# Longformer attention and a softplus MLP: narrow idle products at the start, and weight loads that wait for earlier ones

## The chip, the cores and the metric

The kernel runs on one core of a Trainium2 chip. The metric is device time in microseconds (us): the median over several runs. A separate profiled execution gives the trace from which everything else is read. An instruction is named by its engine and its line in the kernel: PE is TensorE (PEld its weight loads), DVE VectorE, ACT ScalarE, POOL GpSimd, SP SyncE, which here only issues transfers.

## The reference

Batch 8, 8 heads, 576 positions, head size 64, 8 global positions drawn at random; then 4608 tokens of width 512 go through an MLP of width 2048.

```python
mask = np.abs(pos[:, None] - pos[None, :]) <= 32          # a band
mask = mask | is_global[:, None] | is_global[None, :]     # and global rows and columns
attn = softmax(where(mask, q @ k.T / sqrt(64), -1e9))
x = (attn @ v)  -> [4608, 512]
out = softplus(x @ w_in) @ w_out                          # w_in 512 x 2048, w_out 2048 x 512
```

All inputs are float32; the kernel computes in bf16 with float32 sums.

## The kernel before, in words

**Tiling.** The tokens are cut into 9 tiles of 512 (`m`), each tile into 4 groups (`n`) of 4 blocks of 32 positions. For a group, PE computes scores `s` for all 8 heads against the block's own, previous and next block and the global keys (`sc`, L1085), DVE takes the row maxima `m`, ACT the exponentials `st` (L1121 for the first four groups, in pieces of 128 columns), DVE the reciprocal of the sums, POOL or DVE the normalisation `pn` (L1140), DVE a transposition `pt` (L1149), and PE the product with v, `xo` (L1259). ACT and DVE copy `xo` to `xT`. Then PE computes `h` = xT times w_in (L1294, 16 chunks `c` of 128 columns of w_in), ACT the softplus `g` (L1300), and PE the product `o` with w_out (L1305). Of tile 0, `xo` and `h` come in three pieces of 128, 256 and 128 tokens. Once a batch, rows of the global positions are computed apart: `sg` (L976), exponentials `pg` (L988), `ov` (L1005), `vg`.

**Start of the program.** q and k of batches 0 and 1 come in three parts each: part 0 and 1 hold 256 positions (one transfer of 512 KB, L522), part 2 the last 64 (two transfers of 64 KB, L526); they are called q0, q1, q-tail, k0, k1, k-tail here. They are issued on SP's queue. A part is cast to bf16 (`qb`, `kb`), transposed by PE (`tr`, L865, in order q0, q-tail, q1 and k0, k1, k-tail), gathered at the global positions by PE (`pick`, L871), and the transposed tiles are copied to `qx` and `kx`. The scores of the first group need q0, k0 and, through the global keys that ACT copies from `pick`, all of k. v of batch 0 (8 transfers of 72 KB, L477) and w_in (8 transfers of 256 KB, called pieces 0 to 7, two for each of four tiles `win`, L1356) are issued on POOL's queue; they are cast on the way. POOL's queue is in order: an instruction that waits holds those behind it. Two of its instructions do nothing but wait: a copy of one column to `seen`. SP's queue waits in the same way before the loads of batch 1: a tiny transfer `trail` (L765) reads an element of `win`.

**Idle products.** Until PE has work, it multiplies a zeroed tile, `warm` (L737). `keep` puts such products into every gap of over 700 ns that the planner foresees in the first 34 us, and computes their number from a share of the gap and the duration of one.

**What sets the order.** `_Order` plans all jobs with costs written in the code. The table `ORDER` gives the order in which it takes them, five times the job's number plus the engine (0 PE, 1 ACT, 2 DVE, 3 POOL, 4 SP's transfers). The planner's times choose the idle products and sort the jobs; each engine then executes its instructions in that order. It also has a model of PE's instruction fetch (`stall`): blocks of 256 instructions, each asked for when a row of PE's program 318 ahead of its first is reached (`ASK`, `NEED`).

Of the kernel before, what the change touches and what calls it, by code (L numbers as in the profile page):

```python
# [20 lines left out]
class _Order:  # L21
# [16 lines left out]
    SWITCH = 107  # L38
# [4 lines left out]
    SLOW = ((27000, 8000), (34500, 6200), (55000, 8200), (230000, 6000), (1e9, 4500))  # L43
    NEAR = 150

    def stall(self, t, took, ins):
# [4 lines left out]
        while n + ins >= min(asked, need):  # L51
            at = min(asked, need)
            here = t + held + took * max(at - n, 0) / max(ins, 1)
            if at == asked:
                due.append(here)
                asked += self.BLOCK
            else:
                ask = due.pop(0)
                took_ = max(next(x for until, x in self.SLOW if ask < until), self.backlog(ask + 1200) - ask + 2400)
                last = max(ask + took_, last + self.FETCH)  # L60
                held += max(0, last - here)
                need += self.BLOCK
# [48 lines left out]
    BEGIN = 3300  # L111
# [43 lines left out]
    FILL, FILLT, NARROW, NFILL, NFILLT = 0.75, 220, 0, 0.8, 140  # L155
    COLD, COLDT, LONG = 5400, 427, 0.93
# [3 lines left out]
    def keep(self, t0, t1, order):  # L160
# [11 lines left out]
        if t0 < self.COLD:  # L172
            span = (t1 - t0) * self.LONG
# [20 lines left out]
    def due(self, j):  # L194

        t = j["hold"]
        for d in j["deps"]:
            same = d["on"] in j["cost"] and (
                d["on"] == "PE" or d["on"] == "DMA" and (not d["moves"] or not j["moves"] and d["cost"]["DMA"][0])
                or d["on"] == "POOL" and d["moves"])  # L200
# [10 lines left out]
    def run(self, free):  # L211
# [12 lines left out]
        dma = []  # L224
# [3 lines left out]
        while ready:  # L228
# [57 lines left out]
            if j["moves"]:  # L286
                mine = "POOL" if "POOL" in j["cost"] else "SP"
                dma.append((mine, t + 1500 if j["cost"][e][0] else t, j["moves"], j))
# [28 lines left out]
def kernel(  # L317
# [51 lines left out]
    ORDER = (52, 57, 62, 162, 167, 122, 137, 146, 156, 4, 117, 113, 151, 141, 132, 127, 182, 172, 177, 187, 370, 9, 14, 213,  # L369
# [1108 lines left out]
```

## Time and profile before

| | us |
|---|---|
| median of 3 runs (332.8 to 333.18) | 333.17 |
| profiled execution | 331.16 |
| its span, first to last instruction | 329.1 |
| PE busy in the span | 319.9 |
| idle products `warm`: 46, busy | 13.9 |
| first product `xo` of tile 0 starts at | 26.30 |
| first product `h` of tile 0 starts at | 28.20 |

The profiled execution took 2.06 us more than its span, and 2.01 us less than the median of the runs. Rows of the timeline below read: start in us, us, engine, line, operation, output<-inputs, shapes, number of instructions merged; in brackets the idle time of the engine before it and what ended it ("issue": nothing that the profile shows). Rows of the windows read: stretch, its length, busy us of each engine with the number of instructions, then the granted TensorE clock (1.00 is full), the share and the GB/s of the transfers. Rows of a queue read: packets, MB, share of 16 transfer engines' time; q1 carries SP's loads, q0 POOL's transfers, q8 blocks of PE's instructions.

### The profile page before, as it was taken

What the parts mean: (1) busy time and instruction counts of PE and PEld (TensorE: products, weight loads), DVE (VectorE), ACT (ScalarE), POOL (GpSimd) and SP (SyncE); (2) the same over time, 40 slices, a digit from 0 to 9 for tenths busy, and PEclk for the clock granted to TensorE, in tenths of its full rate; (3) what the DMA queues carried; (4) which work ended last, traced back from release to release, by engine and by line L of the source; (5) the groups of instructions that cost most, each with busy time, mean ns of one, the idle gap of its engine ahead of it and who ended that gap; (6) DMA issues with size and microseconds to landing.
All of it is one profiled execution on the core that took longest, in us unless ns stands there. A gap on an engine that the chain in (4) does not pass through costs nothing.

```text
span 329.1 us, 12101 instructions
## 1 busy us (share of the span) xinstructions
PE 319.9 (97%) x5290; PEld 171.3 (52%) x5290; DVE 219.9 (67%) x386; ACT 233.8 (71%) x459; POOL 196.0 (60%) x175
## 2 busy tenths in 40 slices
PE   8878999999999999999999999999999999999996
PEld 3536876565555444544555445445544454454444
DVE  7796689847997799884995975378776970431000
ACT  5698879676798896488558857995749647914622
POOL 7827828996678567969587496738282927230000
PEclk9997999999999999999999999999999999999999
DMA  7998999999889899999999960370010012001002
GB/s 193 187 205 195 198 189 155 157 166 244 136 152 146 152 226 173 180 228 189 178 179 167 155 162 4 127 145 3 4 66 0 36 66 85 13 32 66 34 32 97
DMA packets 168796, 42.14 MB, mean 128 GB/s; under 512 B 153256, under 2 KB 165800, under 8 KB 168744
## 3 DMA queue, kind: packets, MB, share of 16 engines
q1 hardware_dynamic: 155928, 27.15, 46.8%
q0 software_dynamic: 10944, 11.08, 16.9%
q10 hardware_dynamic: 1872, 3.15, 2.5%
q8 instruction: 41, 0.67, 0.9%
q14 instruction: 11, 0.09, 0.1%
HBM read 36.71 MB, written 9.44 MB: 140 GB/s over the span
## 4 chain that ended last, share of the span: by engine, by line
PE 90%; DVE 2%; SPq 2%; DMA 2%; issue 1%; ACT 1%
PE o L1305 39%; PE h L1294 37%; PE xo L1259 4%; PE s L1085 4%; DMA stage<-in_q_dram 2%; PE ov L1005 2%; SPq L522 1%; PE pick L894 1%; SPq L526 1%; PE sg L976 1%; PE warm L737 1%; DVE qx L728 1%; PE tr L865 1%; DVE m L1100 1%; PE pick L907 1%
## 5 line engine op out<-in xcount | busy, mean ns | idle before, releaser
L1305 PE MATMUL o<-wout,g 128*128 128x512 bf16 (+1 forms) x592 | 138.3, 374 | 0.0
L1294 PE MATMUL h<-xT,win 128*128 128x512 bf16 (+3 forms) x768 | 137.8, 328 | 0.1
L1300 ACT ACTIVATE g<-h 128x512 bf16<-128x512 f32 (+3 forms) x192 | 84.5, 503 | 30.0 <-PE h L1294 27.0
L1140 POOL TENSOR_TENSOR pn<-st,rs 128x1024 bf16<-128x1024 f32 (+1 forms) x38 | 66.7, 1766 | 55.7 <-DVE rs L1134 49.9
L1294 PEld LDWEIGHTS <-win 128*128 128x128 bf16 x768 | 67.5, 99 | 59.6 <-issue 0.8
L1305 PEld LDWEIGHTS <-g 128*128 128x128 bf16 x592 | 55.9, 98 | 60.7 <-ACT g L1300 1.0
L1108 POOL TENSOR_TENSOR st<-st,m 128x1024 f32<-128x1024 f32 x32 | 60.2, 1894 | 27.1 <-DVE m L1102 27.0
L1089 DVE TENSOR_TENSOR st<-s,mask 128x512 f32<-128x512 f32 x64 | 41.1, 677 | 18.6 <-PE s L1085 18.4
L1132 DVE TENSOR_REDUCE sm<-st 128x8 f32<-128x1024 f32 x32 | 38.5, 1203 | 14.8 <-ACT st L1125 14.6
L1102 DVE TENSOR_REDUCE m<-st 128x8 f32<-128x1024 f32 x32 | 37.9, 1209 | 0.3
L728 ACT COPY osb<-o 128x512 f32<-128x512 f32 (+1 forms) x30 | 17.2, 577 | 22.6 <-PE o L1305 20.2
L1125 ACT ACTIVATE st<-st 128x1024 f32<-128x1024 f32 x32 | 32.7, 1052 | 0.3
L1149 DVE STREAM_TRANSPOSE pt<-pn 128x512 int32<-128x512 int32 x36 | 24.5, 690 | 5.2 <-POOL pn L1140 5.1
L728 ACT CAST xT<-xo 128x512 bf16<-128x512 f32 (+3 forms) x28 | 11.7, 467 | 18.8 <-PE xo L1259 18.8
L728 DVE CAST xT<-xo 128x512 bf16<-128x512 f32 (+3 forms) x20 | 11.3, 601 | 17.5 <-PE xo L1259 17.4
L1300 ACT ACT_TABLE_LOAD x15 | 19.2, 1283 | 1.7 <-PE h L1294 1.5
L1125 ACT ACT_TABLE_LOAD x14 | 18.0, 1283 | 0.7 <-ACT osb L728 0.4
L725 POOL TENSOR_SCALAR qb<-stage 128x1152 bf16<-128x1152 f32 (+2 forms) x15 | 16.8, 1126 | 2.2 <-issue 1.1
L1085 PE MATMUL s<-kx,qx 64*32 64x128 bf16 x1152 | 14.5, 220 | 3.6 <-issue 2.8
L1085 PEld LDWEIGHTS <-qx 64*32 64x32 bf16 x1152 | 10.4, 90 | 12.2 <-issue 8.9
L728 POOL CAST vb<-stage 128x1152 bf16<-128x1152 f32 x12 | 13.7, 1146 | 3.3 <-DMA stage<-in_v_dram 3.3
L737 PE MATMUL warm<-vb 128*128 128x512 bf16 x46 | 13.9, 451 | 1.3 <-DVE vb L559 1.3
(127 smaller groups left out, 287.2 us busy)
## 6 DMA issues: line engine op xcount, KB each, us to landing
stage<-in_v_dram SPq DMA_DIRECT2D x56, 144.0 KB, 4.2
stage<-in_q_dram SPq DMA_DIRECT2D x48, 144.0 KB, 3.7
stage<-in_k_dram SPq DMA_DIRECT2D x48, 144.0 KB, 4.0
out_dram<-osb POOLq DMA_DIRECT2D x24, 256.0 KB, 3.2
out_dram<-osb ACTq DMA_DIRECT2D x11, 256.0 KB, 2.0
stage<-in_q_dram SPq DMA_DIRECT2D x4, 512.0 KB, 6.2
stage<-in_k_dram SPq DMA_DIRECT2D x4, 512.0 KB, 6.9
win<-in_moe_w_in_dram POOLq DMA_DIRECT2D x8, 256.0 KB, 7.7
```

What stands on the lines that cost most here:

```text
L728: {"ACT": nc.scalar.copy, "DVE": V.tensor_copy, "POOL": nc.gpsimd.tensor_copy}[e](out, in_)
L1085: nc.tensor.matmul(out=PS["s", n, g][quad(a), x, :], lhsT=qx[b % 2][rows(g), a, j * BL:(j + 1) * BL], rhs=kx[b % 2][rows(g), a, e0 * BL:(e ...
L1089: V.tensor_tensor(out=PS["st", n][:, h, :, :], in0=PS["s", n, h][:, :, :], in1=mask[:, h, j0:j0 + PB, :, :].rearrange("p j s i -> p j (s i ...
L1102: V.reduce_max(out=m[:], in_=flat(PS["st", n], h0, h1), axis=AX)
L1108: on(e).tensor_tensor(out=t, in0=t, in1=over(PS["m", n, y][:], SL * BL), op=OP.subtract)
L1125: nc.scalar.activation(out=t, in_=t, func=AF.Exp)
L1132: V.reduce_sum(out=sm[:], in_=flat(PS["st", n], h0, h1), axis=AX)
L1140: on(e).tensor_tensor(out=PS["pn", n][:, :, :, h0:h1].rearrange("p x s h -> p h x s"), in0=PS["st", n][:, h0:h1], in1=PS["rs", n, y][:].re ...
L1149: V.transpose(out=bass.AP(base.tensor, base.offset, ap=[list(base.ap[0]), [2 * STEP, PB // 2], [STEP + BL // 2, 2], [1, SL * BL]]), in_=PS ...
L1294: nc.tensor.matmul(out=h[:, :], lhsT=w_in_t[c // 4][:, kd, c % 4 * P:(c % 4 + 1) * P], rhs=PS["xT", m][:, kd, lo:hi], start=(kd == 0), sto ...
L1300: nc.scalar.activation(out=PS["g", m, c][:, lo:hi], in_=PS[key][:, lo_of(c, hi - lo)], func=AF.Softplus)
L1305: nc.tensor.matmul(out=PS["o", m, ns, a][:, :], lhsT=PS["g", m, kf][:, ns * P:(ns + 1) * P], rhs=w_out_t[kf // 4][:, kf % 4, a:z], start=( ...
```

## The change

1. The idle products of a gap that begins before 3 us are 128 columns wide instead of 512: the first series is 156 of 128 columns instead of 29 of 512.
2. POOL waits for k1 (a copy to `seen`) before it issues the first v.
3. Each of w_in's pieces 4 to 7 waits for the landing of the piece four before it, by a copy of one column of `win` to `seen` on POOL; the planner's fixed hold of 2000 ns on these transfers is gone.
4. SP's loads of batch 1 wait for the first piece of win2 (piece 4) instead of its second; w_out waits for k0 of batch 1 instead of k1.
5. Several of the planner's costs are changed, and `ORDER` is another table.

```diff
-    SWITCH = 107
+    SWITCH = 96
-    SLOW = ((27000, 8000), (34500, 6200), (55000, 8200), (230000, 6000), (1e9, 4500))
+    SLOW = ((27000, 6500), (36500, 5500), (50000, 7500), (230000, 5800), (1e9, 4500))
-    BEGIN = 3300
+    BEGIN = 2900
-    FILL, FILLT, NARROW, NFILL, NFILLT = 0.75, 220, 0, 0.8, 140
-    COLD, COLDT, LONG = 5400, 427, 0.93
+    FILL, FILLT, NARROW, NFILL, NFILLT = 0.75, 220, 3000, 0.93, 57
+    COLD, COLDT = 5400, 107
...
-                dma.append((mine, t + 1500 if j["cost"][e][0] else t, j["moves"], j))
+                dma.append((mine, t + (1900 if mine == "POOL" else 1500) if j["cost"][e][0] else t, j["moves"], j))
...
-    ORDER = (52, 57, 62, 162, 167, 122, 137, 146, 156, 4, 117, 113, 151, 141, 132, 127, 182, 172, 177, 187, 370, 9, 14, 213,
+    ORDER = (24, 29, 73, 78, 83, 88, 57, 176, 181, 62, 67, 152, 187, 192, 157, 14, 138, 217, 162, 197, 202, 312, 147, 33,
...
+    DEPTH = 4
...
-    seen = const([P, 2, 1], FP32, "seen")
+    seen = const([P, 10, 1], FP32, "seen")
...
+            last = o.add(pool(190), lambda e: nc.gpsimd.tensor_copy(seen[:, 2, :], natural(1, 1)[:, 0, 0, 0, 0:1]), [T["part", 0, 1, 1]], rank=0)
...
-            T["part", b, w, t] = o.add({"DMA": (700 if b else 0, 0)}, emit, had(("w_in", 2)) + T["cast", 0, w] if b else [], rank=0,
+            T["part", b, w, t] = o.add({"DMA": (700 if b else 0, 0)}, emit, had(("w_in", 2, 0)) + T["cast", 0, w] if b else [], rank=0,
...
+    pieces = []
     for x in range(4):
         for y in range(2):
-            last = T["w_in", x] = o.add({"POOL": (650, 0)}, lambda e, x=x, y=y: weights_in(x, y), [last or T["held"]],
-                                        rank=-1 if x else 0, hold=2000 if x else 0, moves=1340)
+            gate = []
+            if len(pieces) >= DEPTH:
+                n = len(pieces) - DEPTH
+                gate.append(o.add(pool(190), lambda e, n=n: nc.gpsimd.tensor_copy(seen[n % 2 * D:n % 2 * D + D, 4 + n, :], w_in_t[n // 2][n % 2 * D:n % 2 * D + D, 0, 0:1]), [pieces[n]], rank=0, late=1))
+            last = T["w_in", x] = T["w_in", x, y] = o.add({"POOL": (650, 0)}, lambda e, x=x, y=y: weights_in(x, y), [last or T["held"], *gate],
+                                        rank=-1 if x else 0, moves=1340)
+            pieces.append(last)
```

What the new table does to the order is seen best on two queues. First SP's queue, the first loads of the program. The transfers from `in_q_dram` and `in_k_dram` of 128x8x128 are parts 0 and 1, those of 64x4x64 the tails. Before:

```order
L531 DMA gi_63<-in_global_idx_dram 128x16
L522 DMA stage0_60<-in_q_dram 128x8x128
L522 DMA stage1_61<-in_k_dram 128x8x128 x2
L522 DMA stage0_60<-in_q_dram 128x8x128
L526 DMA stage1_61<-in_k_dram 64x4x64 x2
L526 DMA stage0_60<-in_q_dram 64x4x64 x2
L765 DMA trail_111<-win2_126 1x2x1
```

With the change:

```order
L533 DMA gi_63<-in_global_idx_dram 128x16
L528 DMA stage0_60<-in_q_dram 64x4x64 x2
L524 DMA stage0_60<-in_q_dram 128x8x128
L524 DMA stage1_61<-in_k_dram 128x8x128 x2
L524 DMA stage0_60<-in_q_dram 128x8x128
L528 DMA stage1_61<-in_k_dram 64x4x64 x2
L767 DMA trail_111<-win2_126 1x2x1
```

By the table's numbers the parts came as q0, k0, k1, q1, k-tail, q-tail, and come now as q-tail, q1, k1, k0, q0, k-tail. PE's order of transposes still begins with q0.

Second POOL's queue behind its first constants, up to the normalisation. Before:

```order
L725 TENSOR_SCALAR qb_64<-stage0_60 128x2x4x64
L477 DMA vb0_66<-in_v_dram 32x18x64 x8
L1373 COPY seen_110<-stage0_60 128x1
L1356 DMA win0_124<-in_moe_w_in_dram 64x4x512 x2
L671 COPY mask_78<-mask_78 128x2x256
L1356 DMA win1_125<-in_moe_w_in_dram 64x4x512 x2
L1356 DMA win2_126<-in_moe_w_in_dram 64x4x512 x2
L1356 DMA win3_127<-in_moe_w_in_dram 64x4x512 x2
L1140 TENSOR_TENSOR pn_735<-st_415,rs_680 128x512
```

With the change, up to the gate of piece 6:

```order
L1376 COPY seen_110<-stage0_60 128x1
L1359 DMA win0_124<-in_moe_w_in_dram 64x4x512 x2
L1359 DMA win1_125<-in_moe_w_in_dram 64x4x512
L667 MEMSET mask_78 128x9x32 x4
L775 COPY seen_110<-stage1_61 128x1
L478 DMA vb0_66<-in_v_dram 32x18x64 x2
L649 TENSOR_SCALAR mask_78<-near_120 128x2x9x8 x2
L730 CAST kb_65<-stage1_61 128x2x4x64
L478 DMA vb0_66<-in_v_dram 32x18x64 x2
L1383 CAST seen_110<-win0_124 64x1 x2
L478 DMA vb0_66<-in_v_dram 32x18x64 x2
L1359 DMA win1_125<-in_moe_w_in_dram 64x4x512
```

Three pieces of w_in are now issued ahead of v, and as soon as q1 has landed; the eight transfers of v are spread in pairs, the last two pairs behind the landing of pieces 0 and 1. Behind these rows come the last pair of v, the gates on pieces 2 and 3 and the issue of pieces 4 to 7, and then six normalisations `pn`. On ACT, the exponentials of groups 1 and 2 stand ahead of the first copy of `xT`, those of group 3 behind it, and then softplus; the product `vg` moves from ACT to DVE. PE has 12 idle products of 512 columns in later gaps (9 and 3) instead of 17 in six series.

More of the change, by code (lines that the diff above doesn't have):

```diff
@@ L58, in stall @@
                 ask = due.pop(0)
-                took_ = max(next(x for until, x in self.SLOW if ask < until), self.backlog(ask + 1200) - ask + 2400)
+                took_ = max(next(x for until, x in self.SLOW if ask < until), self.backlog(ask + 1400) - ask + 2400)
                 last = max(ask + took_, last + self.FETCH)
@@ L172, in keep @@
         if t0 < self.COLD:
-            span = (t1 - t0) * self.LONG
+            span = (t1 - t0) * share
             cold = min(span, self.COLD - t0)
@@ L199, in due @@
                 d["on"] == "PE" or d["on"] == "DMA" and (not d["moves"] or not j["moves"] and d["cost"]["DMA"][0])
-                or d["on"] == "POOL" and d["moves"])
+                or d["on"] == "POOL" and d["moves"] and (j["moves"] or not j["late"]))
             t = max(t, j["hold"] + (d["at"] if same else d["end"] + self.HOP))
@@ L759, with follow @@
     followed = set()
-    def follow(x, t):
+    def follow(x, t, row):
         if x in followed:
@@ L764, in follow @@
         followed.add(x)
-        nc.sync.dma_start(out=trail[x:x + 1, :], in_=t[D:D + 1, t.shape[1] - 1, t.shape[2] - 2:])
+        nc.sync.dma_start(out=trail[x:x + 1, :], in_=t[row:row + 1, t.shape[1] - 1, t.shape[2] - 2:])
     def add_load(b, w, deps):
@@ L775, in add_load @@
                     last = T["half", 0, h] = o.add({"POOL": (1300, 0)}, lambda e, h=h, x=x: load_v(nc.gpsimd, 0, h, range(2 * x, 2 * x + 2)), [last], rank=0,
-                                                   moves=1200, late=200)
+                                                   moves=1080, late=200)
                     T["cast", 0, 2].append(last)
@@ L782, in emit @@
                     if behind:
-                        follow(1, w_out_t[0])
+                        follow(1, w_out_t[0], D)
                     load_v(nc.sync, b, h, range(R))
@@ L795, in emit @@
                 if b:
-                    follow(0, w_in_t[2])
+                    follow(0, w_in_t[2], 0)
                 load_part(b, w, t)
-            T["part", b, w, t] = o.add({"DMA": (700 if b else 0, 0)}, emit, had(("w_in", 2)) + T["cast", 0, w] if b else [], rank=0,
-                                       moves=(1800 if b else 1900) if t < FULL else 900 if b else 650, units=1 if t < FULL else 2)
+            T["part", b, w, t] = o.add({"DMA": (700 if b else 0, 0)}, emit, had(("w_in", 2, 0)) + T["cast", 0, w] if b else [], rank=0,
+                                       moves=1800 if t < FULL else 900 if b else 650, units=1 if t < FULL else 2)
     def add_cast(b, w):
@@ L1042, in add_global @@
             ovs.append(o.add({"PE": (72 * n, 72 * n + 170) if b else (110 * n + 100, 110 * n + 240)}, lambda e, m0=m0, m1=m1: ov(e, m0, m1), [tps[-1], *ovs, *T["cast", b, 2]],
-                             rank=3, array=32, ins=16 * n, opens=[] if ovs else [("ov", ("ov", b, y)) for y in range(two)], uses=[("ov", b, y) for y in range(two)] if ovs else []))
+                             rank=3, array=34, ins=16 * n, opens=[] if ovs else [("ov", ("ov", b, y)) for y in range(two)], uses=[("ov", b, y) for y in range(two)] if ovs else []))
         T["gexp", b], T["tpg", b], T["ov", b] = exps[-1], tps[-1], ovs[-1]
@@ L1275, in add_values @@
             last = o.add({"PE": (t, t + 170)}, lambda e, s0=s0, s1=s1: val(e, s0, s1), ready if last is None else [last] + (had(("gv", 0)) if ahead else []),
-                         rank=1, array=64, urgent=last is None, ins=16 * (s1 - s0) + (8 if ahead and s0 == 0 else 0), opens=opened if last is None else [],
+                         rank=1, array=65, urgent=last is None, ins=16 * (s1 - s0) + (8 if ahead and s0 == 0 else 0), opens=opened if last is None else [],
                          uses=[("pt", m)] + ([("xo", v_, r) for r in range(KD)] if last is not None else []))
@@ L1436 @@
             make_batch(1)
-            T["landed"] = o.add(pool(100), lambda e: nc.gpsimd.tensor_copy(seen[:, 0, :], natural(1, 1)[:, 0, 0, 0, 0:1]), [T["part", 1, 1, 1]], rank=0)
+            T["landed"] = o.add(pool(100), lambda e: nc.gpsimd.tensor_copy(seen[:, 0, :], natural(1, 0)[:, 0, 0, 0, 0:1]), [T["part", 1, 1, 0]], rank=0)
             for a in range(KF // 4):
                 T["w_out", a] = o.add({"POOL": (800, 0)}, lambda e, a=a: weights_out(a),
-                                      [T["landed"], T.get(("w_out", a - 1))], rank=-1, hold=800 if a else 0, moves=2700)
+                                      [T["landed"], T.get(("w_out", a - 1))], rank=-1, moves=2700)
         for x in range(len(VALS)):
```

143 rows, old and new, of the table ORDER are left out of this document.

## The prediction

> **What bounds the kernel now.** I read the page first, then stretches of the span, then the first 40 us engine by engine, then the transfer queues.
>
> ```profile
> PE 319.9 (97%) x5290; PEld 171.3 (52%) x5290; DVE 219.9 (67%) x386; ACT 233.8 (71%) x459; POOL 196.0 (60%) x175
> ...
> 23.30:26.14 2.84, 0.00 (x2) 0.00 (x1) 2.13 (x8) 2.84 (x17) 0.62 (x1) 1.00 1.16 194
> 26.14:30.00 3.86, 3.86 (x74) 2.89 (x75) 2.10 (x6) 2.79 (x17) 3.42 (x4) 0.56 0.69 185
> 30.00:34.34 4.34, 4.34 (x141) 3.75 (x139) 3.20 (x7) 3.94 (x17) 2.65 (x3) 1.00 0.91 214
> 34.34:326.00 291.66, 291.26 (x4732) 154.09 (x4728) 193.59 (x309) 207.84 (x361) 173.94 (x130) 1.00 0.62 120
> ```
>
> PE bounds it. From 34.34 us on PE is idle 0.40 us in 291.66, so the time is the moment at which PE becomes full plus a fixed rest. All that can be won lies ahead of that moment: PE stands still for 2.84 us, and for the next 3.86 us has a clock of 0.56, which loses 3.86 x 0.44 = 1.7 us.
>
> ```profile
> 22.89 0.41 PE L1085 MATMUL s<-kx,qx 64*32 64x128 bf16 x30
> 26.14 0.23 PE L1085 MATMUL s<-kx,qx 64*32 64x128 bf16 x2 [2.84 <-issue]
> ...
> 28.20 4.33 PE L1294 MATMUL h<-xT,win 128*128 128x128 bf16 x60
> ...
> 34.34 0.39 PE L865 MATMUL tr<-ident,kb 128*128 128x128 bf16 x4
> ...
> 35.64 2.78 PE L1294 MATMUL h<-xT,win 128*128 128x256 bf16 x24
> ```
>
> The stop is in the middle of one group's scores and waits for nothing in the program. It is at row 704 of PE's program (scores at rows 644 to 707, 30 pairs done), where the planner's model of the instruction fetch has a block begin (448 + 256). The queue of PE's instructions shows one block moved between 23.5 and 24.0 us, none between 17.5 and 23.5:
>
> ```profile
> q8 instruction: 1, 0.02, 11.2%
> ...
> win<-in_moe_w_in_dram POOLq DMA_DIRECT2D x2, 256.0 KB, 9.7
> ```
>
> The second row is the last two of w_in's transfers (issued by 18.41, landing 9.7 us on): all eight had been queued in 6 us, and the block went through among them. I take the stop for that block.
>
> Beside PE runs a second chain, ACT's:
>
> ```profile
> 16.14 0.37 ACT L1121 ACTIVATE st<-s,m 128x128 f32<-128x128 f32 x1
> ...
> 20.31 0.35 ACT L1121 ACTIVATE st<-s,m 128x128 f32<-128x128 f32 x1
> ...
> 27.50 0.60 ACT L728 CAST xT<-xo 128x128 bf16<-128x128 f32 x3 [1.07 <-PE xo L1259]
> 27.98 0.39 ACT L1121 ACTIVATE st<-s,m 128x128 f32<-128x128 f32 x1
> ...
> 30.93 1.28 ACT L1300 ACT_TABLE_LOAD   x1
> 32.23 1.64 ACT L1300 ACTIVATE g<-h 128x128 bf16<-128x128 f32 x9
> 34.23 0.37 ACT L728 CAST xT<-xo 128x256 bf16<-128x256 f32 x1 [0.38 <-PE xo L1259]
> ```
>
> From the first exponential at 16.14 ACT is nearly full up to softplus; it lost only 1.07 us to PE's stop. So removing the stop does not give 4.5 us: ACT comes next.
>
> **The change part by part.** Call E the start of the first exponential. With the change ACT does, in order: group 0 and the global rows (16.14 to 20.31, 4.17), groups 1 and 2 (20.31 to 26.43 less `vg`, now on DVE: 5.9), two copies of xT (0.4), group 3 (27.98 to 30.93: 2.9), the table (1.28), four softplus (4 x 1.64/9 = 0.7), two copies of 256 columns (0.6). That is 16.0 us; then PE can begin `h` of 256 columns, at E + 16.0. Before, it began at 35.64, behind four groups of transposes of batch 1 in 1.30 us; the new order has only two ahead of it, so the equal point is 35.64 - 0.65 = 34.99. The gain is 34.99 - 16.0 - E = 19.0 - E. PE itself would be ready: `xo` of group 0 waits for POOL's normalisation behind w_in's last issue. Here is its price, and how long POOL needs to issue six pieces:
>
> ```profile
> 14.73 3.68 POOL L1356 DMA_DIRECT2D win<-in_moe_w_in_dram  x6
> 25.52 4.04 POOL L1140 TENSOR_TENSOR pn<-st,rs 128x512 bf16<-128x512 f32 x4 [7.11 <-DVE rs L1134]
> ```
>
> Piece 3 is issued behind the landing of piece 1 (14.9 by the packet rates below) and two issues of v (5.59 / 8 each), at 16.5. Landed at some 21, then three issues of 0.61: the first `pn` at 23, `xo` at 26, before ACT is at the copies (E + 10.1). This cover is about 2 us; if w_in's gates open later than that, every further us is lost. The gates and the fetch go together: with at most some four pieces outstanding the block no longer meets eight, PE does not stop for it, and the clock has no gap of 2.84 us. I cost the gates' copies (0.2 each on POOL) at nothing under the same cover, and the three added changes of tile shape on PE at 0.3 at most.
>
> So everything hangs on E, and E on two loads. The first parts became usable like this:
>
> ```profile
> 5.54 0.63 ACT L721 ACTIVATE qb<-stage 128x512 bf16<-128x512 f32 x1 [0.65 <-DMA stage<-in_q_dram]
> ...
> 7.35 1.14 ACT L728 CAST kb<-stage 128x512 bf16<-128x512 f32 x2 [1.18 <-DMA stage<-in_k_dram]
> ...
> 9.18 1.14 ACT L728 CAST kb<-stage 128x512 bf16<-128x512 f32 x2 [0.69 <-DMA stage<-in_k_dram]
> ...
> 12.69 0.74 DVE L728 COPY qx<-tr 128x512 bf16<-128x512 bf16 x1 [0.22 <-PE tr L865]
> ...
> 14.85 0.46 PE L1085 MATMUL s<-kx,qx 64*32 64x128 bf16 x32
> ...
> 15.41 1.29 DVE L1100 TENSOR_REDUCE m<-s 128x4 f32<-128x512 f32 x2
> ...
> L728 DVE CAST kb<-stage x4: 273/418/1275, 13.3 to 33.6; 128x512 bf16<-128x512 f32 x3, 128x256 bf16<-128x256 f32 x1
> ```
>
> (The last row groups the casts by DVE: least, median and longest in ns.) One part per 1.8 us. Now q-tail goes ahead (two transfers, 0.8 together), and q0, which PE's transposes need first, is fourth of the large ones: 5.54 + 0.8 + 3 x 1.8 = 11.8. Behind q0: two casts on DVE (0.85), first transposes (0.85), a copy (0.74), a cast (0.4), two copies (1.5), scores (0.46), maxima (0.65), hops: 5.7. So undisturbed loads give E = 17.5, against 16.14 before: the first exponential is later than now in any case. The gain is then 1.5.
>
> The loads are not undisturbed: w_in's pieces 0 to 2 are issued from 6.6 us, when k0, q0 and k-tail are still to come. What POOL's transfers do to SP's is seen in five stretches, from 8 to 9, 9 to 10, 10 to 11, 54 to 55 and 56 to 57 us:
>
> ```profile
> q1 hardware_dynamic: 580, 0.29, 120.4%
> ...
> q1 hardware_dynamic: 526, 0.27, 109.4%
> q0 software_dynamic: 100, 0.01, 20.0%
> ...
> q0 software_dynamic: 655, 0.08, 129.7%
> q1 hardware_dynamic: 353, 0.10, 58.0%
> ...
> q0 software_dynamic: 8, 0.01, 7.0%
> ...
> q0 software_dynamic: 130, 0.13, 91.1%
> q1 hardware_dynamic: 165, 0.02, 23.6%
> ...
> 6.17 5.59 POOL L477 DMA_DIRECT2D vb<-in_v_dram  x8
> ```
>
> The first v, issued at 6.17, had its first packets only at about 9.85, and until then SP's loads ran at full speed. By that delay of 3.7 piece 0 moves from 10.3 on, when k0 is through and 220 of q0's 1024 packets are left. From there the two queues take packets about one for one, as at 56 us (a w_out transfer against loads of q: 165 a us for SP): q0 lands 0.9 later than undisturbed, k-tail's 512 packets take 3.2 and land near 15.8; cast, transposes, global keys, scores and maxima put E at 19.0. The gain is then 0. I take E = 18.2, between the two, since v took fewer of SP's packets than one for one in the one stretch that lies at this place (353 a us were left): gain 0.8.
>
> **The idle products** cost PE no time while nothing is ready:
>
> ```profile
> 1.26 8.76 PE L737 MATMUL warm<-vb 128*128 128x512 bf16 x29 [1.26 <-DVE vb L559]
> ...
> 5.93 3.60 PEld L737 LDWEIGHTS <-vb 128*128 128x128 bf16 x17 [0.28 <-issue]
> ...
> 50.71 1.28 PE L1294 MATMUL h<-xT,win 128*128 128x128 bf16 x20
> ```
>
> Until 5.93 one took about 0.43, then 0.21 (3.60/17), though the granted clock reads 1.00 throughout. At 128 columns: 0.107, then 0.056 (1.28 less the last one's tail, over 20). 43 slow and 113 fast ones end at 5.9 + 6.3 = 12.2, ahead of q0's first cast transposed at 12.7: nothing. They advance PE's row count by 254, so blocks are asked for earlier; that is part of the fetch's cure.
>
> The other terms lie off the path: loads of batch 1 start up to 2 us earlier, as they wait for piece 4; w_out waits for k0 alone.
>
> **Sum.** 19.0 - 18.2 = 0.8 us: the profiled execution goes from 331.16 to 330.4, and the median, 2.01 above it, to 332.4. "No change" below means within 0.2% (0.67 us), about what a measurement of this kernel can tell.
>
> **Rivals.**
> 1. No change (0.25). The stop is gone, but ACT's chain starts as much later: E from 18.4 to 19.6, time 333.2. For it: q0 and k-tail come behind w_in in time. Against it: v left SP's loads alone up to 9.85.
> 2. Slower, since w_in's first three pieces take SP's packets (0.20). The 3.7 us of the first v may have been its wait for the load under way; a w_out transfer issued at 52.9 had its first 8 packets before 55, about 1.9 later, with SP's loads queued. Then piece 0 moves from 8.5, with 1786 of SP's packets left (250 of k0, q0, tails). While 768 of w_in pass at 150 a us, SP gets about 770, until 13.6; then v's first pair leaves it 290 a us, q0 lands at 16.3, E = 22.0: 3.0 lost, 336.2. It decides from E = 19.0, q0 landing later than 13.3. [...]
> 3. Slower, since PE's clock drops again (0.07). New gaps: 12.2 to 13.5, and some 1.5 before `h`. The same 1.7 comes back: 332.4 + 1.7 = 334.1. For it: a stop of 2.84 was enough; against it: none of the new ones is as long. [...]
> 4. Slower, since narrow idle products don't open the clock (0.04): 156 x 0.107 = 16.7, to 18.0; transposes start 5 late, E about 22.8, 337. Against it: they leave no gap on PE.
> 5. The stop stays and only moves to row 448 (0.02): the block asked for at 10.3 before came through at 17; row 448 is now due at 17 too. Up to 2 us, 334.4.
>
> **How the numbers follow.** The forecast, faster by over 0.67, has 0.42: E below 18.3, times from 331.1 to 332.5; its upper reach is E = 17.5 with 0.5 more from PE's fuller start. No change 0.25; slower 0.20 + 0.07 + 0.04 + 0.02 = 0.33. The range goes from 330.4 (a gain of 2.8, beyond every term but PE's own 4.5) to 335.9, just short of rival 2's full price, so that about 2 in 10 stay out.
>
> **What would show it.** Right: no PE wait on "issue" of over 1 us before 35 us, granted clock 1.00 from 20 to 34, first exponential at 18.2, `h` of 256 columns at about 34.2, PE idle at most 0.5 after that. Wrong: q0's cast later than 13.3 or E later than 19.0; packets of q0 (POOL's queue) before 9 us beside fewer than 400 of q1's; first `pn` on POOL after 25; a clock under 1 before 34; or an ACT lag that keeps PE waiting for banks between 35 and 44.

## The result: 3.4% slower, with stops at places far apart

The changed kernel takes 344.15 us (median), the kernel before in the same series 332.99. The ratio is 1.0342, with a 95% interval from 1.0284 to 1.0400. The forecast was 332.4 with a range up to 335.9. Medians below are over all runs of a kernel, while the ratios leave out single runs over 1.5% above the fastest of the same kernel (one each of the changed kernel, e5, e7 and e8; that of e7 took 1778 us).

The profiled execution took 343.29 us, 12.1 more than that of before. First the page of the changed kernel, then stretches of its span (columns as before):

```profile
PE 320.3 (94%) x5368; PEld 180.2 (53%) x5412; DVE 230.6 (68%) x402; ACT 229.1 (67%) x446; POOL 193.6 (57%) x177
```

```profile
15.00:20.00 5.00, 4.11 (x81) 3.41 (x79) 1.78 (x3) 2.18 (x5) 4.33 (x10) 0.66 1.76 141
...
30.00:35.00 5.00, 2.81 (x60) 1.49 (x61) 3.10 (x9) 3.71 (x23) 2.31 (x3) 0.77 1.09 275
...
32.04:34.40 2.36, 2.21 (x53) 0.89 (x54) 1.49 (x5) 1.53 (x9) 0.28 (x1) 0.65 1.13 294
...
76.97:80.70 3.73, 0.07 (x2) 0.10 (x1) 3.68 (x7) 1.08 (x1) 0.91 (x1) 0.98 0.77 139
80.70:100.00 19.30, 18.65 (x397) 10.97 (x400) 16.70 (x26) 12.25 (x23) 10.68 (x9) 0.92 0.65 126
100.00:338.00 238.00, 233.94 (x3586) 118.16 (x3616) 150.43 (x235) 165.98 (x254) 130.32 (x90) 1.00 0.50 105
```

Two things show here: PE stands still more, at places far apart, and behind such places the clock is lower. One thing must be read with care: 5412 weight loads stand beside 5368 products, so 44 products have no record, and each leaves a false gap (of 0.16 us for 512 columns). Most of the 4.06 us without a product in the last row above is of that kind; in the profile of before both counts are 5290. PE's work has not grown, apart from idle products: 5412 less 168 idle ones and 5290 less 46 are both 5244. Its busy time has, though 320.3 us beside 319.9 hides it for want of the 44: e9 below, whose trace has all of the same 5412, shows 327.1. An estimate for the changed kernel from its own rows comes near the same: 319.9, three more stretches of 3.4 us at half clock (1.7 each) and 1.6 more of idle products are 326.6.

The timeline of the changed kernel, PE first, has the four places that matter:

```profile
1.26 10.86 PE L739 MATMUL warm<-vb 128*128 128x128 bf16 x156 [1.26 <-DVE vb L561]
14.79 0.40 PE L868 MATMUL tr<-ident,qb 128*128 128x128 bf16 x4 [2.67 <-DVE qb L725]
...
20.86 0.56 PE L1088 MATMUL s<-kx,qx 64*32 64x128 bf16 x32 [1.35 <-DVE kx L730]
...
32.04 0.28 PE L1248 MATMUL xo<-vb 128*128 128x128 bf16 x2 [2.05 <-ACT st L1124]
...
40.46 2.17 PE L1297 MATMUL h<-xT,win 128*128 128x256 bf16 x16
...
80.70 0.55 PE L1262 MATMUL xo<-pt,vg 32*64 32x384 bf16 x8 [3.66 <-DVE pt L1152]
```

`h` of 256 columns starts at 40.46 in place of 35.64: 4.8 us are lost up to there. From there to the end of the span it is 301.1 us in place of 293.5: another 7.7, where the prediction had no term at all.

The first exponential, E in the prediction, comes at 22.25. Its chain on ACT and DVE:

```profile
10.74 0.62 ACT L730 CAST kb<-stage 128x512 bf16<-128x512 f32 x1 [5.42 <-DMA stage<-in_k_dram]
17.16 0.41 ACT L730 CAST kb<-stage 128x256 bf16<-128x256 f32 x1 [5.80 <-DMA stage<-in_k_dram]
17.47 0.72 ACT L730 COPY qx<-tr 128x512 bf16<-128x512 bf16 x1
...
22.25 0.37 ACT L1124 ACTIVATE st<-s,m 128x128 f32<-128x128 f32 x1 [1.29 <-DVE m L1103]
...
13.51 1.22 DVE L725 TENSOR_SCALAR qb<-stage 128x512 bf16<-128x512 f32 x2 [1.34 <-DMA stage<-in_q_dram]
18.22 0.73 DVE L730 COPY qx<-tr 128x512 bf16<-128x512 bf16 x1 [3.49 <-ACT qx L730]
```

ACT stands still from 11.4 to 17.16, until k-tail has landed. The copies of q0's transposes, which PE had made by 15.7, are queued behind that cast, and DVE's copies behind ACT's.

The queues of the changed kernel from 10 to 11, 11 to 12 and 13 to 14 us show what k-tail waited for (q1 are SP's loads, q0 POOL's transfers, q8 a block of PE's instructions):

```profile
q1 hardware_dynamic: 566, 0.29, 119.1%
...
q0 software_dynamic: 109, 0.11, 68.5%
q1 hardware_dynamic: 261, 0.13, 52.6%
q8 instruction: 1, 0.02, 7.2%
...
q0 software_dynamic: 156, 0.16, 93.9%
q1 hardware_dynamic: 145, 0.04, 28.2%
```

Issued at 7.28, w_in's pieces move from 11.15 on, 3.9 us later. Then SP's packets fall from 566 to about 150 a us, with k-tail's 512 still to come.

### The profile page after: what moved, and what is told of

It is laid out like the page before. It is cut to its first block, busy times and chain, and to the rows that moved or that the text cites. A ratio compares the mean times of both kernels' runs of the same rounds, so it can differ in the third digit from the quotient of the medians.

```text
span 341.6 us, 12301 instructions
## 1 busy us (share of the span) xinstructions
PE 320.3 (94%) x5368; PEld 180.2 (53%) x5412; DVE 230.6 (68%) x402; ACT 229.1 (67%) x446; POOL 193.6 (57%) x177
## 3 DMA queue, kind: packets, MB, share of 16 engines
HBM read 36.71 MB, written 9.44 MB: 135 GB/s over the span
## 4 chain that ended last, share of the span: by engine, by line
PE 78%; ACT 8%; DVE 6%; DMA 2%; issue 2%; SPq 2%; DVEq 0%; ACTq 0%
PE h L1297 33%; PE o L1308 33%; PE xo L1262 4%; PE s L1088 3%; DMA stage<-in_k_dram 2%; ACT st L1124 2%; ACT g L1303 2%; PE ov L1008 1%; SPq L524 1%; PE pick L897 1%; ACT st L1128 1%; DVE sm L1135 1%; DVE pick L603 1%; SPq L528 1%; ACT L1303 1%
## 5 line engine op out<-in xcount | busy, mean ns | idle before, releaser
L1308 PE MATMUL o<-wout,g 128*128 128x512 bf16 (+1 forms) x560 | 133.5, 374 | 3.6 <-issue 2.4
L730 ACT CAST xT<-xo 128x512 bf16<-128x512 f32 (+3 forms) x27 | 11.4, 473 | 22.0 <-PE xo L1262 21.9
L730 ACT COPY osb<-o 128x512 f32<-128x512 f32 (+1 forms) x24 | 13.6, 568 | 16.7 <-PE o L1308 11.7
L730 DVE CAST xT<-xo 128x512 bf16<-128x512 f32 (+3 forms) x21 | 11.4, 570 | 16.8 <-PE xo L1262 16.8
L730 ACT CAST kb<-stage 128x1152 bf16<-128x1152 f32 (+2 forms) x9 | 11.5, 1276 | 11.3 <-DMA stage<-in_k_dram 11.2
L739 PE MATMUL warm<-vb 128*128 128x128 bf16 (+1 forms) x168 | 15.5, 264 | 1.3 <-DVE vb L561 1.3
L727 POOL TENSOR_SCALAR qb<-stage 128x1152 bf16<-128x1152 f32 (+2 forms) x12 | 14.1, 1187 | 2.1 <-PE h L1297 1.1
```

Of the source, the lines that this page charges most:

```text
L730: {"ACT": nc.scalar.copy, "DVE": V.tensor_copy, "POOL": nc.gpsimd.tensor_copy}[e](out, in_)
L1308: nc.tensor.matmul(out=PS["o", m, ns, a][:, :], lhsT=PS["g", m, kf][:, ns * P:(ns + 1) * P], rhs=w_out_t[kf // 4][:, kf % 4, a:z], start=( ...
```

## The experiments

All ratios are to the kernel before on the same chip. E is the first exponential, `h` the first product of 256 columns; both are of the profiled execution, in us.

| kernel | median, us | ratio, 95% interval | E | h |
|---|---|---|---|---|
| changed kernel | 344.15 | 1.0342, 1.0284 to 1.0400 | 22.25 | 40.46 |
| before + narrow idle products (e1) | 342.17 | 1.0312, 1.0224 to 1.0399 | 18.00 | 37.81 |
| the same, blocks where they were (e6) | 334.95 | 1.0072, 1.0045 to 1.0100 | 18.07 | 39.04 |
| before + gates (e2) | 331.84 | 0.9996, 0.9966 to 1.0026 | 16.21 | 36.54 |
| changed, pieces 0 to 2 later (e3) | 344.25 | 1.0362, 1.0314 to 1.0410 | 19.11 | 42.35 |
| changed, picking table early (e4) | 346.44 | 1.0432, 1.0388 to 1.0475 | 22.36 | 42.67 |
| changed, k-tail's cast behind (e5) | 344.69 | 1.0342, 1.0260 to 1.0425 | 21.14 | 38.90 |
| changed, wide idle products (e7) | 345.92 | 1.0392, 1.0328 to 1.0456 | 22.04 | 41.40 |
| changed, no gates (e8) | 344.11 | 1.0333, 1.0279 to 1.0387 | 22.32 | 38.38 |
| changed, three edits (e9) | 343.88 | 1.0335, 1.0240 to 1.0430 | 22.06 | 40.42 |
| changed, four edits (e10) | 338.72 | 1.0187, 1.0115 to 1.0259 | 19.55 | 36.84 |

### Part 1 alone (e1_narrow)

```diff
-    FILL, FILLT, NARROW, NFILL, NFILLT = 0.75, 220, 0, 0.8, 140
-    COLD, COLDT, LONG = 5400, 427, 0.93
+    FILL, FILLT, NARROW, NFILL, NFILLT = 0.75, 220, 3000, 0.93, 57
+    COLD, COLDT = 5400, 107
...
-            span = (t1 - t0) * self.LONG
+            span = (t1 - t0) * share
```

> The kernel before with part 1 of the change alone: the first idle products are 116 of 128 columns in place of 29 of 512, and PE's program has 194 rows more. Theory A (the loss of the change lies in its table of the order, not in the idle products): within 1 us of the kernel before, 332.0 to 334.2, no granted clock under 1 before 20 us, first exponential within 0.3 of 16.1. Theory B (narrow products do not hold the clock): a clock of 0.5 somewhere before 20 us, the first exponential later by 1 us or more, 334.5 or more. For the stop of PE: if a block that begins at row 704 is the cause, it is met 194 rows earlier in the work or is gone; if the stop stays at the same scores (the 30th pair of its group), the row count was not its cause.

It made the kernel before 3.1% slower, nearly as much as the whole change. The timeline of PE in that kernel shows where:

```profile
139.19 0.91 PE L1259 MATMUL xo<-pt,vb 32*64 32x64 bf16 x88
143.01 0.38 PE L1305 MATMUL o<-wout,g 128*128 128x512 bf16 x1 [2.91 <-issue]
...
273.82 0.36 PE L1259 MATMUL xo<-pt,vb 32*64 32x64 bf16 x21
276.39 0.20 PE L1259 MATMUL xo<-pt,vb 32*64 32x32 bf16 x3 [2.21 <-issue]
```

Two new stops, far behind every idle product, and behind each the clock is halved for 3.4 us (1.7 lost): the granted clock of this execution is 0.97 over 140 to 200 us and 0.98 from 200 us on, where that of before is 1.00 in both. Both lie at rows of PE's program where a block of 256 rows begins (5568 and 9920, less a few rows by which the boundary drifts). I counted rows by the weight loads in the traces, took the start of the row 318 ahead of a block's first as "asked" (the planner's own figure; the asking itself stands in no trace), and the start of the last weight load ahead of the boundary as "needed"; "moved" is the block's transfer on q8:

```
kernel   block at   asked   needed   room   moved   PE goes on   stop
before      704      17.2     23.0    5.9    23.8      26.14     2.84
e1         5568     138.5    139.9    1.4   140.6     143.01     2.91
e1         9920     271.8    274.0    2.2   273.9     276.39     2.21
changed     960      23.4     29.7    6.3    29.6      32.04     2.05
changed    1472      37.6     43.4    5.8    41.7      44.15     0.46
changed    9920     272.0    277.0    5.0   273.8       -         -
e4          960      23.2     29.5    6.2    30.7      33.15     3.42
e4         1472      39.8     45.1    5.2    45.0      47.45     2.11
e4         9920     270.3    275.4    5.0   275.3     277.76     2.19
```

So every stop in this table is a late block, and PE goes on 2.3 to 2.5 us after the block has begun to move. In the runs below, too, every stop of over 0.3 us named "issue" lies at such a row. The 194 rows added (87 idle products more in the first series and 10 in later gaps, two rows each) shifted the blocks of the whole program against the work. In the order of before the least room behind 100 us is 4.5 us; in e1 it is 1.4, since 318 rows of short products pass in that time there. The wait of 2.05 us in the changed kernel, which the timeline gives to ACT, is one of these too: it lies at row 960 and ends 2.4 us after the block's move.

The stop of 2.84 us is gone from the 30th pair of its scores, as expected if the row count is its cause; three stops of 0.5 to 0.8 us lie before 53 us in its place. Theory A fails. All three signs of theory B came: a clock of 0.5 from 18.0 us, E at 18.00, more than 334.5. Its cause did not: the narrow products took 0.106 us each, and 0.056 from 4.4 us on, as the prediction estimated, so they did reach the fast pace; and the two stops with the half clock behind them are 8.5 us in the profile, where the medians differ by 10.1.

### The same with the blocks at their old places (e6_narrow_aligned)

```diff
+    MORE = 31
...
         for x in range(n):
             nc.tensor.matmul(out=ps[:, 0:w], lhsT=idle[:, 0, :], rhs=idle[:, 0, :] if thin else idle, start=True, stop=True)
+        for x in range(MORE if thin else 0):
+            nc.tensor.matmul(out=ps[:, 0:16], lhsT=idle[:, 0, :], rhs=idle[:, 0, 0:16], start=True, stop=True)
```

> The kernel before with part 1 alone, as in e1_narrow, and behind the first series 31 more idle products of 16 columns, so that PE's program has exactly 256 rows more than before and every block of instructions begins at the same place of the work. Theory A (e1_narrow lost its time because 194 more rows put blocks of instructions behind stretches of short products): the stops of e1_narrow at 143.0 (2.9 us) and 276.4 (2.2) and those at 52 and 36 are gone, the stop before the scores is back at the same 30th pair with 1.5 to 3 us, no other stop over 0.6 behind 60 us, time 333 to 336 (the first exponential at 17.5 to 18.2, as a block moved among SP's first loads holds k-tail up). Theory B (the narrow products cost by themselves): stops of 2 us or more behind 100 us again, 340 to 343.

The median falls from 342.17 to 334.95, the two stops are gone (none over 0.4 us behind 60 us), and the clock is not halved again behind 23 us. The stop of before stands at row 960, which is the old 704, here in the timeline of PE:

```profile
29.45 1.25 PE L738 MATMUL warm<-vb 128*128 128x512 bf16 x5 [1.17 <-issue]
```

Two others of 1.0 and 1.2 us appear at 47.3 and 53.8. Theory A holds, though the stop at row 960 is 1.17 where 1.5 to 3 were expected: of the 3.1%, 2.4 come from the places of the blocks. The 0.7% left goes with the added products themselves: E is 1.9 later than before. In e1 and in e6 the first block moves at 10.4 and 10.7, among SP's loads, where it moved at 17.4 before, and the tail of k lands later, as a row of PE's waits in e1 shows (total, times, longest, in us):

```profile
PE tr L868 <- DVE kb L728: 1.2, 1, 1.2
```

That the block is what holds k-tail up rests on these two kernels against two without it (before and e2); I did not try it by itself.

### The gates alone (e2_gates)

```diff
     def weights_in(x, y):
+        n = 2 * x + y - 4
+        if n >= 0:
+            nc.gpsimd.tensor_copy(seen[n % 2 * D:n % 2 * D + D, 4 + n, :], w_in_t[n // 2][n % 2 * D:n % 2 * D + D, 0, 0:1])
```

> The kernel before with part 3 of the change alone: each of the pieces 4 to 7 of w_in is issued behind the landing of the piece four before it; PE's rows are those of before. Theory A (the stop of 2.84 us comes of a block of instructions that goes through among eight queued pieces): the stop is under 1 us, and the clock has no 0.5 at 26 to 30; since ACT was late by 1.07 us only, the time is 331.5 to 332.9. Theory B (the stop has another cause): it stays at 2.5 to 3 us and the time at 333 or, as the normalisations on POOL come behind the gates, up to 336.

The row of PE's timeline that answers to the stop of before:

```profile
25.31 0.23 PE L1085 MATMUL s<-kx,qx 64*32 64x128 bf16 x2 [1.94 <-issue]
```

The stop is 1.94 in place of 2.84: the block moves at 22.9 in place of 23.8. Neither theory holds for the stop, though the time lies in theory A's range: with at most four pieces outstanding the block still waits 5.6 us from its asking to its move. The 0.9 is given back, since PE then waits 1.1 us for ACT ahead of a transpose and 0.9 for w_out ahead of an `o`. No change in time.

### The changed kernel without gates (e8_no_gates)

```diff
-                gate.append(o.add(pool(190), lambda e, n=n: nc.gpsimd.tensor_copy(seen[n % 2 * D:n % 2 * D + D, 4 + n, :], w_in_t[n // 2][n % 2 * D:n % 2 * D + D, 0, 0:1]), [pieces[n]], rank=0, late=1))
+                gate.append(o.add(pool(190), lambda e, n=n: nc.gpsimd.memset(seen[n % 2 * D:n % 2 * D + D, 4 + n, :], 0.0), [pieces[n]], rank=0, late=1))
```

> The changed kernel without the waits of pieces 4 to 7 of w_in: the four copies on POOL become fills of the same column, so that the pieces are issued as soon as POOL comes to them. Theory A (a block of instructions is held up by the pieces that are queued when it is asked for): with the pieces issued by 19 to 21 us and through by 29, the block that PE waits for near 30 us (row 960, asked for at 23.4, moved at 29.6 in the changed kernel) comes no later, its wait is 1 to 3 us, and the time is within 1 us of the changed kernel. Theory B (the gates are what cures it): the wait grows to 3.5 us or more and the time by 1.5 us or more. The other way round: the wait shrinks under 1 us and the time falls by 2 us, then the gates themselves had put the pieces where the block goes.

The block at row 960 moves 4.1 us after it was asked for in place of 6.2, and the wait there is gone; `h` starts 2.1 earlier. The profiled execution stays 2.3 to 2.7 us ahead of the changed kernel's up to 171 us; then a stop of 1.71 at 173.6 with a halved clock takes 3.5. The median is that of the changed kernel (344.11). So the wait is that of the third case and the time that of theory A: the gates don't cure the fetch in this order. That they delay it, since the last three pieces, held up to 23 us, are issued just when that block is asked for, is argued from one execution of each kernel; the same block took 6.2 and 7.5 us from asking to move in the changed kernel and in e4, which have the same order up to there.

### Pieces 0 to 2 later (e3_pieces_later)

```diff
-    ORDER = (24, 29, 73, 78, 83, 88, 57,
+    ORDER = (24, 29, 57,
...
-             213, 298, 43,
+             213, 298, 73, 78, 83, 88, 43,
```

> The changed kernel with one move in the table: the first three pieces of w_in are issued on POOL behind the wait for k1, the first two transfers of v and the cast of k, some 7 us later than in the changed kernel (7.3 us). The planner adds 14 idle products of 512 columns at places where PE waits for ACT. Theory A (the three pieces took the packets of q0 and k-tail, and everything behind waits for k-tail's cast at 17.16): q0 is cast at 12.4 to 12.8 in place of 13.51, k-tail is cast before 15, the first exponential comes at 18 to 20 in place of 22.25, and the time falls by 2 to 4 us to 340 to 342; more only if the wait of 3.66 us at 80.7 goes with it. Theory B (the parts are late by SP's new order alone): k-tail's cast stays later than 16 and the first exponential later than 21, time 343 to 345.

In the timeline of this kernel, the cast of q0 on DVE, that of k-tail on ACT, and PE's longest wait for w_in:

```profile
12.75 0.80 DVE L725 TENSOR_SCALAR qb<-stage 128x512 bf16<-128x512 f32 x2 [0.70 <-DMA stage<-in_q_dram]
...
14.32 0.41 ACT L730 CAST kb<-stage 128x256 bf16<-128x256 f32 x1 [2.88 <-DMA stage<-in_k_dram]
...
36.56 3.84 PE L1297 MATMUL h<-xT,win 128*128 128x128 bf16 x40 [2.70 <-DMA win<-in_moe_w_in_dram]
```

k-tail is cast 2.8 us earlier and E comes 3.1 us earlier, at 19.11: theory A on the loads. For k-tail that is clear; q0's 12.75 shows little, since e5 and e8, with w_in issued as in the changed kernel, have 12.77 and 12.81. But `h` then waits 3.0 us for w_in, whose gated pieces now come late, and the time stays. DVE's late transposition stops PE for 3.63 us at 81.9 as well, though the start was other: that stop does not come of the late start.

### The table for picking early (e4_pick_early)

The entry 222 of `ORDER` (the job that makes the table for picking) moves from behind 2823 to ahead of 712, that is from 72.9 us on DVE to behind a copy of xT at 45.3. In the timeline of the changed kernel, DVE and POOL ahead of PE's stop at 77 us:

```profile
71.17 3.79 POOL L1143 TENSOR_TENSOR pn<-st,rs 128x1024 bf16<-128x1024 f32 x2 [0.50 <-DVE rs L1137]
74.93 1.48 POOL L727 TENSOR_SCALAR qb<-stage 128x1152 bf16<-128x1152 f32 x1
76.33 1.56 POOL L730 CAST kb<-stage 128x1152 bf16<-128x1152 f32 x1
...
73.14 1.86 DVE L598 TENSOR_SCALAR place<-pos,pi 128x32 bf16<-128x32 f32 x1
73.17 1.83 DVE L599 TENSOR_SCALAR pi<-pi 128x1 f32<-128x1 f32 x1
75.04 0.23 DVE L600 TENSOR_SCALAR posK<-pos,pi 128x18 f32<-128x18 f32 x1
75.31 3.32 DVE L603 TENSOR_TENSOR pick<-posK,gf 32x144 bf16<-32x144 f32 x4
78.64 0.69 DVE L730 COPY osb<-o 128x512 f32<-128x512 f32 x1
79.34 1.30 DVE L1152 STREAM_TRANSPOSE pt<-pn 128x512 int32<-128x512 int32 x2
```

```diff
-             705, 1150, 712, 1250,
+             705, 1150, 222, 712, 1250,
...
-             2838, 2823, 222, 1602,
+             2838, 2823, 1602,
```

> The changed kernel with one move in the table: DVE makes the table for picking (the lines 543, 598 to 603) at about 45.5 us, where POOL has nothing to do, in place of 72.9. Theory A (at 73 us DVE shares something with POOL's normalisations, so that this work takes 5.7 us, and the transposition that PE waits for at 80.7 comes late): this work takes about 2 us, PE's wait of 3.66 us at 77 is under 0.5, the clock has no gap behind it, and the time falls by 4 to 5.5 us, to 338.4 to 340. Theory B (DVE is late at 80 us because everything began 6 us late): another wait of 2 us or more takes its place before 100 us, and the time falls by less than 2 us.

The same instructions in the timeline of this kernel, and then the stretch of its span that held the stop:

```profile
49.10 0.12 DVE L598 TENSOR_SCALAR place<-pos,pi 128x32 bf16<-128x32 f32 x1
49.13 0.14 DVE L599 TENSOR_SCALAR pi<-pi 128x1 f32<-128x1 f32 x1
49.30 0.23 DVE L600 TENSOR_SCALAR posK<-pos,pi 128x18 f32<-128x18 f32 x1
49.57 1.24 DVE L603 TENSOR_TENSOR pick<-posK,gf 32x144 bf16<-32x144 f32 x4
```

```profile
76.00:82.00 6.00, 5.95 (x169) 4.23 (x167) 4.54 (x8) 4.82 (x14) 5.68 (x4) 1.00 0.85 144
```

With POOL idle the two short instructions take 0.12 and 0.14 us in place of 1.86 and 1.83, and the four products of `pick` 1.24 in place of 3.32: in the changed kernel two of the four took 1.20 and 1.47 beside POOL's two casts and ended 0.1 us behind them (at 76.50 and 77.99), the other two 0.30 each. The whole job falls from 5.7 us to 1.9, 1.7 of it by the two and 2.1 by the four, and PE has no stop at 77. Row by row this execution makes up 4.8 us on the changed kernel between 72 and 89 us: theory A, for the place. The time did not fall all the same (346.44): the stops for blocks at the rows 960, 1472 and 9920 were longer in it by 1.4, 1.7 and 2.2 us (table above), with the clock halved behind the first (0.66 over 30 to 40 us) and the last (0.98 from 200 us on), but not behind the second (1.00 over 40 to 60). I had not foreseen that, and the other half of theory A, a fall of 4 to 5.5 us, failed.

### The cast of k-tail behind the copies (e5_tail_cast_behind)

```diff
-             237, 19, 326, 240, 255, 246, 262, 270, 285, 300, 315, 330, 357, 307, 277, 291, 386,
+             237, 19, 240, 255, 246, 262, 270, 285, 300, 315, 357, 307, 277, 291, 326, 330, 386,
```

> The changed kernel with one move in the table: on ACT the cast of k-tail (and on PE its transposes) come behind the first copies of qx and kx in place of ahead of them; PE has three more idle products. Theory A (ACT's queue held these copies until k-tail had landed at 17.16, and DVE's copies behind them): the copy of qx on ACT starts before 16.5 in place of 17.47 and the first exponential at 20.3 to 21.3 in place of 22.25; the time falls by 0.5 to 2 us. Theory B (the chain from k-tail through the global keys sets the start whatever the copies do): the first exponential within 0.5 of 22.25, no change.

The copy of qx starts at 14.55 and E comes at 21.14, 1.1 earlier: theory A by its size at E. From k-tail's cast to E it is now 3.7 us in place of 5.1. The time does not fall (344.69), against theory A: a stop of 2.18 at row 1472 takes it.

### Part 1 undone, blocks kept (e7_wide_aligned)

```diff
-        w = P if thin else 4 * P
+        w = 4 * P
+        n = n - 128 if thin else n
...
-            nc.tensor.matmul(out=ps[:, 0:w], lhsT=idle[:, 0, :], rhs=idle[:, 0, :] if thin else idle, start=True, stop=True)
+            nc.tensor.matmul(out=ps[:, 0:w], lhsT=idle[:, 0, :], rhs=idle, start=True, stop=True)
```

> The changed kernel with part 1 undone: 28 idle products of 512 columns in place of 156 of 128, exactly 256 rows fewer, so that blocks begin at the same places of the work but the first is asked for later. The first series ends near 10 us, some 2 us earlier. Theory A (the block that moves at 11.3 us among the last loads holds q0 and k-tail up, as the one at 10.4 did in e1_narrow): no block moves before 14 us, k-tail's cast is at 15.5 to 16.4 in place of 17.16 and the first exponential at 20.8 to 21.6 in place of 22.25. Theory B (k-tail is late by w_in's packets alone): k-tail's cast stays at 17.0 to 17.6. By either, PE's clock is at half speed at some time between 13 and 20, and the stops behind 60 us stay as in the changed kernel: 342 to 345.

No block moves before 18.6 us, yet k-tail is cast at 16.89 only, and E is 22.04. That is between the two theories' ranges and close to B's: e4 and e8, which load as the changed kernel does, have 17.58 and 17.37, so the early block is worth some 0.3 to 0.7 us at most, and with e3 it is w_in's packets that hold k-tail up in this order. The first gap on PE is 4.5 us, the clock is halved for 13.7 us, and the block that the changed kernel waits for at 32 us costs 2.79 here. The time is no better: narrow or wide makes no difference that these runs could show once the blocks are where they were.

### Three and four edits together (e9_three_undone, e10_four_undone)

e9 has e4, e5 and e8 in one kernel, e10 has e3's move as well; PE's rows are kept by 3 and 12 fewer idle products.

> The changed kernel with three edits together, and as many rows of PE as it has: the table for picking made near 45 us, the cast of k-tail behind the first copies of qx and kx, no waits of pieces 4 to 7. Theory A (the loss is a sum of separate causes, of which these are three): no wait of PE for DVE's transposition near 80 us, first exponential at 20.5 to 21.5, PE's stop near 30 us under 1 us; the time falls by 5 to 9 us to 335 to 339. Theory B (what one edit frees is lost again in stops for blocks of instructions, as when the table for picking alone was moved): stops with nothing named of 4 us or more in all, 341 to 345.

> As the run with three edits, and the first three pieces of w_in issued behind the first pair of v and the cast of k as well (at about 12.6 us in place of 7.2), the rows of PE's program kept by 12 fewer idle products in the first series. Theory A (sum of separate causes): k-tail cast before 15 us, first exponential at 17.5 to 19, no wait of h for w_in over 1 us as the pieces no longer wait for each other; 333 to 336. Theory B: w_in comes late for h as when the pieces alone were moved (3.0 us of waits), or stops for blocks eat the gain: 337 or more.

e9 stays at 343.88. In its profile q0 was cast at 14.81, later by 1.3 than in the changed kernel though its loads are the same, and E is 22.06; the stops at rows 960, 1472 and 9920 are 1.8, 2.0 and 2.1 us: theory B. e10 falls to 338.72, which wins back somewhat under half of the loss (1.0342 to 1.0187). That is theory B by its time: k-tail is cast at 16.02 and E is 19.55, both later than theory A had them, and though `h` does not wait for w_in, stops for blocks remain. The stretches of its span up to 100 us show a full clock throughout:

```profile
0.00:30.00 30.00, 24.96 (x481) 18.75 (x481) 21.43 (x68) 16.48 (x63) 21.91 (x51) 1.00 1.11 172
30.00:60.00 30.00, 28.07 (x643) 22.44 (x643) 26.48 (x54) 22.92 (x79) 16.03 (x21) 1.00 1.07 203
60.00:100.00 40.00, 40.00 (x781) 23.30 (x780) 35.21 (x59) 30.11 (x62) 30.52 (x21) 1.00 0.93 166
```

E is 19.55, `h` at 36.84. Its profile is 7.0 us above that of before: `h` is 2.0 later at full run (37.67), stops of 0.46, 0.34, 0.86 and 1.71 us follow, and the two groups of transposes that now lie behind `h` are 0.65. That leaves about 1 us that I did not follow. e10 has 0.6 us of stops at row 960 and none at 1472, where e9 has 1.8 and 2.0; how much of the 5 us between the two is owed to the pieces and how much to blocks that came in time was not separated. Nor was part 2 or part 4 undone alone, or the changed code run with the old table. No kernel here beats the one before.

## Why the prediction was wrong

The forecast (faster by 0.8, through E = 18.2) fell at several of its steps.

**"The loads": a size.** q0 was cast at 13.51, past the 13.3 given as the limit; in e4, e5, e7, e8 and e9, whose first loads are issued in the same order, it was cast at 12.77 to 14.81, so that limit could not decide. Sharing once w_in's packets came was right, "when k0 is through" too. The delay of 3.7 us from issue to first packets came out at 3.9, but partly by luck. Its row was read wrongly: v's first packets of before came at 9.65, not 9.85, which makes 3.5. And it is no fixed time: in e3 and e10 POOL's first transfer was issued at 9.44 and 9.56, and its packets came at 11.72 and 11.56, after 2.3 and 2.0. What sets it stays open. The loads also started later than "two transfers, 0.8 together" said: q1 was usable at 7.16, not at 6.34. And k-tail was cast at 17.16, where I had "near 15.8". e3 shows that w_in's three pieces are the cause: without them ahead it was cast at 14.32.

**From k-tail to E: a step left out.** The sum let 3.2 us pass between k-tail and the first exponential. It was 5.1, since ACT's cast of k-tail stands ahead of the copies of qx and kx in ACT's queue. I had counted the cast as one term and not asked what was queued behind it; e5 gives it 1.1 us at E. Rival 2 named E = 22.0 and a time of 336.2. E came out at 22.25, though not by its early packets (piece 0 moved from 11.15, not from 8.5), so that its E came near is luck, and its time was 8 us short.

**"E + 16.0": a size.** It was 18.2 in the changed kernel, 17.3 to 18.1 in e10. In the first, 2.05 is the wait for the block at row 960, behind which the clock was halved.

**"The block no longer meets eight, PE does not stop for it": wrong in its mechanism.** The stop of before had the cause that I gave it (row 704, the block's move at 23.8). But fewer outstanding pieces shorten it by 0.9 only (e2), and here the gates moved the last pieces to where a later block was asked for (e8; as a cause, argued). Rival 5 looked for the stop at row 448 and gave it 0.02; it came at row 960, with 2.05 and half a clock.

**"The idle products cost PE no time" and "that is part of the fetch's cure": wrong, and dear in the old order.** In time they did hide, ending at 12.1 as worked out. As rows they don't: in the order of before they cost 3.1%, and 0.7% where the blocks are kept (e1, e6). The change escaped the worst of this, since its table goes with its own number of rows (least room behind 100 us: 5.0), so this explains little of its loss; it shows that the count of rows is part of the order.

**"PE full plus a fixed rest": the step that failed worst.** It took all that lies behind 35 us to be unchanged, though `ORDER` is new to the end. 7.7 us were lost there. 3.66 are the stop behind the picking table and 1.7 the clock that it halves (3.4 us at half speed, 80.5 to 83.9); e4 shows the cause. The rest is the two groups of transposes (0.65), stops of 0.46 at row 1472 and 0.61 at 148.5, and about 0.6 that I can't name. The order of DVE around 73 us was there to be read in the new table: a job that stood at 39.6 us had moved behind 70. Instructions of DVE that last longer beside POOL's were not among what I priced: place<-pos,pi took 1.86 us there and 0.12 in e4. It ended within 0.05 us of the end of POOL's two products, at 75.0, and two products of `pick` ended 0.1 us behind POOL's casts, so the rows look like a wait for POOL's instructions; what DVE and POOL share there, no run here shows.

**"Loads of batch 1 start up to 2 us earlier": wrong, at a small price.** They were first issued at 26.70 in place of 26.14, 0.6 later.

Rival 3 (the clock) was named with one price of 1.7. It was paid four times (the granted clock is at half for 3.4 us from 15.7, 22.5, 32.7 and 80.5), against once before.

## What to carry to other kernels

Where an order is given by a table that was made for one number of rows, rows added at the start are not free even where they hide in time: in e1, 194 added rows moved every later block of instructions against the work, and the two blocks that then began right behind many short products (rows 5568 and 9920, with 1.4 and 2.2 us of room in the table above) stopped the engine for 2.91 and 2.21 us. Before trusting "only the start changes", compare the new order to the end of the program, engine by engine, for jobs that now run beside other work: here a job that took DVE 1.9 us in e4 took 5.7 beside POOL's normalisations and casts. And a part that lands late costs what is queued behind its first reader, not only what reads it (1.1 us at E in e5).

## What the runs showed of the hardware that was not expected

PE went on 2.2 to 3.0 us after the late block had begun to move, at every such stop in all these kernels, mostly after 2.3 to 2.5. From asking, as the planner's 318 rows place it, to move it took 1.0 to 7.5 us, and it was not the same in two executions with the same rows: the block at row 9920 moved 1.8 us after its asking in the changed kernel (no stop) and 5.0 in e4 (2.19). What decides between these stays open, as does when a block is really asked for. The rows of the stops in the table (704, 960, 1472, 5568 and 9920) lie whole multiples of 256 apart, as in the planner's model, and one block cost up to 3.42 us (row 960 in e4).

The clock was halved behind some stops and not behind others. In the changed kernel it was behind 2.67 and 2.05 us (granted 0.50 from 15.7 and from 32.7), and the half clock from 22.5 there has only a stop of 1.35, which ended at 20.86, shortly ahead of it. It was behind 1.71 us in e8 at 173.6 (granted clock 0.978 over the whole span of 342.4 us, which is 7.5 us lost), but not behind a stop of the same 1.71 in e10 at 169.2, nor behind one of 2.13 at 14.0 there (1.00 over the whole span), nor behind the 2.11 in e4 at 47.45. What decides this, no run here shows.
